# Reordering a kernel's start: x products ahead of the first weight products, w_in by blocks of columns, two blocks begun on half of x, and two transposes in a shared buffer

## The chip, the core and the metric

The kernel runs on one core of a Trainium2 chip. The time is the device time of one execution in microseconds (us), as a median of several runs. TensorE (PE in the profile) multiplies matrices out of SBUF into PSUM; VectorE (DVE), ScalarE (ACT) and GpSimd (POOL) work on elements; SyncE (SP) issues most transfers (DMA). GpSimd issues the transfers that cast from f32 to bf16. In the traces here each engine does its work in the order of its own queue, and that order is what this study is about.

## The reference, cut to what matters

```python
q_s = softmax(q over its last axis);  k_s = softmax(k over the sequence)   # q, k, v: (8, 8, 576, 64)
kv  = einsum('bhsd,bhse->bhde', k_s, v)
x   = einsum('bhsd,bhde->bhse', q_s, kv)  # seen as 4608 tokens x 512
h   = x @ w_in                            # w_in: 512 x 2048
g   = h + sin(alpha * h)**2 / alpha
out = g @ w_out                           # w_out: 2048 x 512, out: 4608 x 512 f32
```

The kernel goes through nine token blocks of 512. Eight batches of 576 tokens feed them, so the first token block needs batch 0 except its ninth row group, and the second token block needs that group and most of batch 1. Within a token block there are 16 column blocks of 128 columns of w_in, numbered `ni` from 0; below, "block" with such a number is one of these. "The first w_in products" are those of the first token block.

## The kernel before

What the change and the argument touch. First the loads that GpSimd issues at the start: v's second half for batch 0, then w_in, first by rows:

```python
load0(GP, "v", v, 1, 0, 5)
load0(GP, "v", v, 1, 5, 9)
load_win(0, 512, slice(0, 2))       # columns 0-511, half of the rows: two transfers
load_win(0, 512, slice(2, 4))       # the other half of the rows
for c0 in (512, 1024, 1536):
    load_win(c0, c0 + 512)          # 512 columns, all rows, two transfers each
for c in range(2):
    load_wout(c)
```

Then TensorE's order for the first token block. `mm_h(t, ni, _, k0, k1)` adds row groups k0 to k1 of w_in to block ni; `attn_chunk` is an x product; `xT` is x, transposed, in bf16:

```python
kv_mm(0, 1, ps_e, split=True)       # kv of batch 0, second half
kv_norm(0, 1, 2)                    # VectorE: kbd, which the x products read
for ni in range(4):
    mm_h(0, ni, None, 0, 1)         # four w_in products on the first quarter of x
xp = [ps_e.tile(...) for _ in range(2)]
for e in range(2):                  # second half's x products, then casts to xT
    attn_chunk(0, 2 + e, 0, 8, xp[e])
    (DVE_CP, ACT_CP)[e](xT[:, 2 + e, 0:MF], xp[e])
for ni in range(4):
    mm_h(0, ni, None, 1, 2)         # the second quarter
# ... then each block's remaining row groups, its sine, its square and g
```

And the place, after the first token block, where batch 1 is prepared between the output products (`take(os, n)` emits n of them):

```python
for ii in range(2):
    q_transpose(1, ii, ps_e, DVE_CP)
tp = ps_e.tile([128, 2, 128], BF16, name="tp", tag="a")      # a third transpose buffer
for ii in range(2):
    nc.tensor.transpose(tp[:, ii], A["qe", 0][:, 8, ...], identb)
DVE_CP(A["qT", 0][:, :, 8], tp)
cast_v(1, [ACT_CP, DVE_CP])         # VectorE casts v's second half here ...
take(os, 6)
xp = ps_e.tile([128, 4, P], F32, name="xp", tag="a")
# ... the ninth row group's x products ...
DVE_CP(xT[:, :, 8 * P:9 * P], xp)   # ... ahead of this copy, and of an output copy inside take()
take(os, 2)
kv_mm(1, 0, ps_e, split=True);  kv_norm(1, 0, 1);  take(os, 2)
kv_mm(1, 1, ps_e, split=True);  kv_norm(1, 1, 2);  take(os, 1)
```

The softmax here doesn't subtract the row's maximum and nothing guards it: scores larger than these inputs give would overflow.

Of the kernel before, what the change touches and what calls it, by code (L numbers as in the profile page):

```python
# [16 lines left out]
BF16 = mybir.dt.bfloat16  # L17
# [6 lines left out]
def kernel(  # L24
# [14 lines left out]
    nc = tc.nc  # L39
# [5 lines left out]
    J = 9  # L45
# [20 lines left out]
    identb = singles.tile([128, 128], BF16, name="identb")  # L66
    xT = singles.tile([128, 4, NT], BF16, name="xT")
    win = singles.tile([128, 4, d_ff], BF16, name="win")
# [10 lines left out]
    win_v = moe_w_in.rearrange("(x c d) n -> x d c n", x=2, c=4)  # L79
# [5 lines left out]
    def load(name, t, b, halves=False, eng=nc.sync, gate=None):  # L85

        st = stage.tile([128, 4, J, D], F32, name=f"st_{name}", tag="st")
        for ii in range(2) if gate else ():
            gate(st[:, ii, 0, 0:1], zero)
        view = src_view(t, b)  # L90
        flat = st.rearrange("p i j d -> p i (j d)")
        if halves:
            for ii in range(2):
                eng.dma_start(out=flat[:, ii::2], in_=view[:, ii::2])
        else:
            eng.dma_start(out=flat, in_=view)
        staged[name, b] = st
# [3 lines left out]
        load("k", k, b)  # L101
        load("v", v, b)

    def load_win(c0, c1, ks=slice(0, 4)):
        n = slice(c0, c1)
        for x in range(2):
            nc.gpsimd.dma_start(out=win[64 * x:64 * x + 64, ks, n], in_=win_v[x][:, ks, n])

    def load_wout(c):
        nc.gpsimd.dma_start(out=wout[:, 4 * c:4 * c + 4, :], in_=wout_v[:, 4 * c:4 * c + 4, :])  # L110


    A = {}

    def exp_to(dst, src, iis=range(2)):
        for ii in iis:
            nc.scalar.activation(dst[:, :, ii * 128:(ii + 1) * 128].rearrange("p j (x d) -> p x j d", x=2),  # L117
                                 src[:, ii::2], AX.Exp)
# [10 lines left out]
    def exp_k(b):  # L129
        A["ke", b] = att2.tile([128, J, 4 * D], BF16, name="ke")  # L130
        exp_to(A["ke", b], staged["k", b])
# [43 lines left out]
    def kv_norm(b, i0=0, i1=2):  # L175

        kt, m = kbd[b % 2], i1 - i0
        kvr = small.tile([128, 2, 2, 2], F32, name="kvr")[:, :, 0:m]
        src = A["kvp", b][:, :, i0 * 130:i1 * 130].rearrange("p e (ii x c) -> p e ii x c", ii=m, x=2)
        nc.vector.reciprocal(kvr, src[:, :, :, :, D])  # L180
        for x in range(2):
            r = slice(64 * x, 64 * x + 64)
            nc.vector.tensor_tensor(kt[r, :, i0:i1, r], src[r, :, :, x, 0:D],
                                    kvr[r, :, :, x].unsqueeze(3).to_broadcast([64, 2, m, D]), op=ALU.mult)

    def q_tile(b):
        if ("qT", b) not in A:
            A["qT", b] = att2.tile([128, 2, J, 128], BF16, name="qT")
        return A["qT", b]

    def q_transpose(b, ii, pool, eng):
        tp = pool.tile([128, 16, 128], BF16, name="tp", tag="a")
        q_transpose_ii(b, ii, 0, J, tp)
        eng(q_tile(b)[:, ii], tp[:, 0:J])

    def q_transpose_ii(b, ii, j0, j1, tp):

        for j in range(j0, j1):
            nc.tensor.transpose(tp[:, j - j0], A["qn", b][:, ii, j], identb)
# [35 lines left out]
    def mm_h(t, ni, wide=None, k0=0, k1=4):  # L235

        if ni == 0 and k0 == 0:
            G[t] = gpool.tile([128, nN, MF], BF16, name="g")
        if k0:
            hp = HP[t, ni]  # L240
        elif wide and (ni in (4, 5, 9, 10, 14, 15) if t == 0 else ni % 6 in (4, 5)):
            hp = wide()
        else:
            hp = ps_h.tile([128, MF], F32, name="hp", tag="h")
        HP[t, ni] = hp
        for ki in range(k0, k1):
            nc.tensor.matmul(hp, win[:, ki, ni * 128:(ni + 1) * 128],  # L247
                             xT[:, ki, t * MF:(t + 1) * MF], start=(ki == 0), stop=(ki == 3))
        return hp

    def sine(t, ni, hp, sq):
        s = spool.tile([128, MF], F32, name="s")
        nc.scalar.activation(s, hp, AX.Sin, scale=alpha_sb[:, ni:ni + 1])  # L253
        if sq == "A":
            nc.scalar.activation(s, s, AX.Square)  # L255
        elif sq == "P":
            nc.gpsimd.tensor_tensor(s, s, s, op=ALU.mult)  # L257
        else:
            nc.vector.tensor_tensor(s, s, s, op=ALU.mult)
        return s  # L260
# [19 lines left out]
    ACT_CP, DVE_CP, GP_CP = nc.scalar.copy, nc.vector.tensor_copy, nc.gpsimd.tensor_copy  # L280
# [4 lines left out]
    def load0(eng, n, t, ii, j0=0, j1=J):  # L285
        eng.dma_start(out=staged[n, 0][:, ii::2, j0:j1].rearrange("p i j d -> p i (j d)"),
                      in_=src_view(t, 0)[:, ii::2, j0 * D:j1 * D])
# [14 lines left out]
    ps_e = ES.enter_context(tc.tile_pool(name="ps_e", bufs=2, space=PSUM, reuse_waits="tile"))  # L302
# [14 lines left out]
    GP_CP(singles.tile([128, 1], F32, name="held"), staged["k", 0][:, 0, 0, 0:1])  # L317
    load0(GP, "v", v, 1, 0, 5)
    load0(GP, "v", v, 1, 5, 9)
    load_win(0, 512, slice(0, 2))  # L320
    load_win(0, 512, slice(2, 4))
    for c0 in (512, 1024, 1536):
        load_win(c0, c0 + 512)
    for c in range(2):
        load_wout(c)

    def warm_up(n):

        for _ in range(n):
            nc.tensor.matmul(warm, identb, A["qe", 0][:, 0:4, 0:128], start=True, stop=True)  # L330




# [25 lines left out]
    ACT_CP(xT[:, 1, 0:MF], xp[1])  # L360
    kv_mm(0, 1, ps_e, split=True)
    kv_norm(0, 1, 2)
    for ni in range(4):
        mm_h(0, ni, None, 0, 1)
    xp = [ps_e.tile([128, 2, MF], F32, name="xp", tag="a")[:, 0] for _ in range(2)]
    for e in range(2):
        attn_chunk(0, 2 + e, 0, 8, xp[e])
        (DVE_CP, ACT_CP)[e](xT[:, 2 + e, 0:MF], xp[e])
    for ni in range(4):
        mm_h(0, ni, None, 1, 2)  # L370

    def h_slot(t, ni, sq, lag, wide=None):
        hp = mm_h(t, ni, wide, 2 if ni < (4, 2, 0)[min(t, 2)] else 0)
        lag.append((t, ni, hp, sine(t, ni, hp, sq)))

    def flush(lag, keep):
# [23 lines left out]
    with ES:  # L400
        def lent():
            return ps_e.tile([128, 2, MF], F32, name="hh", tag="a")[:, 0]

        def load_q8():
            for ii in range(2):
                load0(nc.sync, "q", q, ii, 8, 9)

        late = {4: load_q8, 6: lambda: load("q", q, 1, halves=True, gate=DVE_CP), 8: lambda: load_wout(2),
                10: lambda: load_wout(3), 13: lambda: load("k", k, 1, halves=True, gate=DVE_CP)}
        for ni in range(nN):  # L410
            h_slot(0, ni, "DPPAPPAPPPAPPAPP"[ni], lag, lent)
            flush(lag, 1)
            if ni in late:
                late[ni]()
        flush(lag, 0)

        accs = [ps_h.tile([128, dm], F32, name="hp", tag="h") for _ in range(4)]
        os = o_quad(0, accs, [DVE_CP, ACT_CP, DVE_CP, ACT_CP])
        take(os, 46)
        exp_to(A["qe", 0][:, 8:9], staged["q", 0][:, :, 8:9])  # L420
        exp_q(1)
        load("v", v, 1, halves=True)
        load_batch(2)
        norm_q8()
        norm_q(1, [GP, V])
        exp_k(1)
        for ii in range(2):
            q_transpose(1, ii, ps_e, DVE_CP)
        tp = ps_e.tile([128, 2, 128], BF16, name="tp", tag="a")
        for ii in range(2):  # L430
            nc.tensor.transpose(tp[:, ii], A["qe", 0][:, 8, ii * 128:(ii + 1) * 128], identb)
        DVE_CP(A["qT", 0][:, :, 8], tp)
        cast_v(1, [ACT_CP, DVE_CP])
        nc.scalar.activation(zero, zero, AX.Sin)
        take(os, 6)
        xp = ps_e.tile([128, 4, P], F32, name="xp", tag="a")
        for c in range(4):
            attn_chunk(0, c, 8, 9, xp[:, c])
        DVE_CP(xT[:, :, 8 * P:9 * P], xp)
        take(os, 2)  # L440
        kv_mm(1, 0, ps_e, split=True)
        kv_norm(1, 0, 1)
        take(os, 2)
        kv_mm(1, 1, ps_e, split=True)
        kv_norm(1, 1, 2)
        take(os, 1)

        c0 = J * P
        for ii in range(2):
            xp = ps_e.tile([128, 2, 512], F32, name="xp", tag="a")[:, :, 0:7 * P]  # L450
            for e in range(2):
                attn_chunk(1, 2 * ii + e, 0, 7, xp[:, e])
            (ACT_CP, DVE_CP)[ii](xT[:, 2 * ii:2 * ii + 2, c0:c0 + 7 * P], xp)
            take(os, 2)
        take(os)
        load("q", q, 3)
        load("k", k, 3)

        for ki in range(2):
            for ni in range(2):  # L460
                mm_h(1, ni, lent, ki, ki + 1)
        for ni in range(nN):
            h_slot(1, ni, SQ[ni], lag, lent)
            flush(lag, 1)
        cast_v(2, [GP_CP, GP_CP])
        flush(lag, 0)
# [38 lines left out]
    c0 = J * 2 * P  # L505
# [33 lines left out]
    for t in range(3, nT):  # L539
# [13 lines left out]
        for ni in range(nN):  # L553
            hp = mm_h(t, ni)
# [46 lines left out]
```

## Time and profile before

| | before |
|---|---|
| median of the first three runs | 289.59 us (289.34 to 290.04) |
| span of the profiled execution | 287.8 us |
| TensorE busy | 273.6 us, 95% |
| first w_in product of the second token block | 48.24 us |
| span left from there | 239.55 us |

The last two rows are the measure that I use throughout. I look for the change's effect ahead of the second token block's first product. I call its start S.

Two lines of VectorE's timeline (start, length, engine, line, operation):

```profile
43.76 0.68 DVE L273 COPY o<-hp 128x512 f32<-128x512 f32 x1
44.36 0.41 DVE L439 CAST xT<-xp 128x256 bf16<-128x256 f32 x1
```

Both stand in VectorE's queue behind the cast of v's second half. That cast could not begin before v had landed at 43.06 us.

### The profile page before, as it was taken

How to read it: one execution, taken by the hardware profiler on the slowest of the kernel's cores; microseconds unless marked ns; L12 is line 12 of the kernel's file. 1: busy time of each engine (PE TensorE's matmuls, PEld its weight loads, DVE VectorE, ACT ScalarE, POOL GpSimd, SP SyncE). 2: the span in 40 equal slices, each digit the busy share in tenths (PEclk: the TensorE clock that was granted, in tenths of full speed). 3: DMA queues.
4: the chain of work that ended last, by engine and by line, in shares of the span. 5: the costliest groups of instructions: out<-in, count | busy, mean ns of one | idle time of the engine just before them, and what ended most of it. 6: DMA issues, size and time to landing. Idle time of an engine off the chain costs nothing.

```text
span 287.8 us, 4238 instructions
## 1 busy us (share of the span) xinstructions
PE 273.6 (95%) x1541; PEld 130.9 (45%) x1569; DVE 189.1 (66%) x285; ACT 225.8 (78%) x319; POOL 81.9 (28%) x77
## 2 busy tenths in 40 slices
PE   2898999999999999999999999999999999999995
PEld 1443454444454445444544454445444444444443
DVE  3947876889958567856776676747674555555412
ACT  4878855999579999899889988999877777777500
POOL 2869520675675662005300440022000000000000
PEclk9999999999999999999999999999999999999999
DMA  7999999945899957119910990115111111111142
GB/s 245 307 204 235 270 396 408 319 159 143 206 144 407 403 178 138 38 38 353 295 23 22 328 344 7 38 39 130 25 39 36 36 36 39 36 36 38 40 109 73
DMA packets 37541, 45.77 MB, mean 159 GB/s; under 512 B 16512, under 2 KB 20880, under 8 KB 37520
## 3 DMA queue, kind: packets, MB, share of 16 engines
q1 hardware_dynamic: 32848, 40.57, 46.1%
q0 software_dynamic: 4480, 4.79, 9.5%
q8 instruction: 12, 0.20, 0.3%
q10 hardware_dynamic: 192, 0.14, 0.2%
q14 instruction: 9, 0.07, 0.1%
HBM read 36.71 MB, written 9.44 MB: 160 GB/s over the span
## 4 chain that ended last, share of the span: by engine, by line
PE 85%; DMA 5%; DVE 3%; POOL 3%; issue 2%; ACT 1%; SPq 0%
PE hp L247 36%; PE op L267 34%; PE hp L267 5%; PE hh L247 2%; PE kvp L170 2%; DMA win<-in_moe_w_in_dram 2%; DMA st_k<-in_k_dram 2%; PE xp L219 2%; POOL s L257 1%; DMA qT<-qn 1%; ACT s L253 1%; PE op L571 1%; PE op L247 1%; DVE qs L149 1%; PE xp L227 1%
## 5 line engine op out<-in xcount | busy, mean ns | idle before, releaser
L263 DVE SCALAR_TENSOR_TENSOR g<-s,inva_sb,hp 128x512 bf16<-128x512 f32 x130 | 96.2, 745 | 64.0 <-ACT s L255 54.2
L247 PE MATMUL hp<-xT,win 128*128 128x512 bf16 x512 | 129.3, 379 | 1.9 <-DMA win<-in_moe_w_in_dram 1.4
L267 PE MATMUL op<-wout,g 128*128 128x512 bf16 x479 | 121.8, 379 | 1.1 <-issue 0.5
L253 ACT ACTIVATE s<-hp,alpha_sb 128x512 f32<-128x512 f32 x130 | 87.5, 683 | 26.9 <-PE hp L247 24.6
L247 PEld LDWEIGHTS <-win 128*128 128x128 bf16 x576 | 56.1, 98 | 70.0 <-issue 2.1
L267 PEld LDWEIGHTS <-g 128*128 128x128 bf16 x560 | 54.0, 98 | 61.6 <-issue 0.7
L255 ACT ACTIVATE s<-s 128x512 f32<-128x512 f32 x111 | 69.9, 630 | 3.5
L151 POOL TENSOR_TENSOR qn<-qe,qs 128x1152 bf16<-128x1152 bf16 x12 | 25.3, 2127 | 72.7 <-DVE qs L145 63.2
L257 POOL TENSOR_TENSOR s<-s 128x512 f32<-128x512 f32 x30 | 31.5, 1060 | 24.9 <-ACT s L253 24.4
L273 DVE COPY o<-op 128x512 f32<-128x512 f32 (+2 forms) x33 | 22.1, 668 | 9.6 <-PE op L267 5.5
L117 ACT ACTIVATE ke<-st_k 128x1152 bf16<-128x1152 f32 x16 | 17.9, 1151 | 4.2 <-DMA st_k<-in_k_dram 4.2
L117 ACT ACTIVATE qe<-st_q 128x1152 bf16<-128x1152 f32 (+2 forms) x18 | 18.0, 1048 | 2.6 <-DMA st_q<-in_q_dram 2.6
L144 DVE TENSOR_REDUCE qs<-qe 128x36 f32<-128x2304 bf16 x5 | 12.8, 2552 | 8.7 <-ACT qe L117 8.6
L136 POOL CAST vb<-st_v 128x1152 bf16<-128x1152 f32 x12 | 13.6, 1162 | 9.9 <-DMA st_v<-in_v_dram 9.9
L267 PE MATMUL hp<-wout,g 128*128 128x512 bf16 x62 | 14.7, 379 | 0.2 <-issue 0.2
L222 DVE CAST xT<-xp 128x512 bf16<-128x512 f32 (+1 forms) x18 | 13.4, 742 | 0.0
L247 PE MATMUL hh<-xT,win 128*128 128x512 bf16 x39 | 9.5, 379 | 0.8 <-DVE g L263 0.7
L170 PEld LDWEIGHTS <-ke 64*128 64x128 bf16 x288 | 8.2, 93 | 4.5 <-issue 1.8
L117 ACT ACT_TABLE_LOAD x7 | 9.0, 1283 | 1.3 <-PEq L585 1.2
L170 PE MATMUL kvp<-vb,ke 64*128 64x130 bf16 x288 | 9.9, 216 | 0.0
L149 DVE TENSOR_REDUCE qs<-qe 128x18 f32<-128x1152 bf16 (+1 forms) x6 | 7.7, 1286 | 2.4 <-ACT qe L117 2.4
L219 PE MATMUL xp<-qT,kbd 128*128 128x256 bf16 (+1 forms) x40 | 8.2, 286 | 0.4 <-DVE xT L222 0.3
(75 smaller groups left out, 119.0 us busy)
## 6 DMA issues: line engine op xcount, KB each, us to landing
out_dram<-o SPq DMA_DIRECT2D x70, 128.0 KB, 2.4
st_q<-in_q_dram SPq DMA_DIRECT2D x6, 1152.0 KB, 6.5
st_k<-in_k_dram SPq DMA_DIRECT2D x6, 1152.0 KB, 8.3
st_v<-in_v_dram SPq DMA_DIRECT2D x6, 1152.0 KB, 10.1
st_k<-in_k_dram SPq DMA_DIRECT2D x4, 576.0 KB, 7.3
wout<-in_moe_w_out_dram POOLq DMA_DIRECT2D x4, 512.0 KB, 11.0
st_v<-in_v_dram SPq DMA_DIRECT2D x3, 576.0 KB, 9.0
win<-in_moe_w_in_dram POOLq DMA_DIRECT2D x6, 256.0 KB, 8.0
```

The source lines that it names most:

```text
L117: nc.scalar.activation(dst[:, :, ii * 128:(ii + 1) * 128].rearrange("p j (x d) -> p x j d", x=2), src[:, ii::2], AX.Exp)
L136: engs[ii](vv[:, 2 * ii:2 * ii + 2, :, 0:D], staged["v", b][:, ii::2])
L151: engs[ii % len(engs)].tensor_tensor(qn[:, ii, 0:j1].rearrange("p j (x d) -> p j x d", x=2), qe[:, ii], part.unsqueeze(3).to_broadcast([12 ...
L170: nc.tensor.matmul(kvp[:, e, ii * 130:(ii + 1) * 130], ke[r, j, ii * 128:(ii + 1) * 128], vt[r, j, ii * 130:(ii + 1) * 130], start=(j == 0 ...
L219: nc.tensor.matmul(xp[:, e, 0:n], kt[:, e, ii], qT[:, ii, j0:j1, e * 64:(e + 1) * 64], start=True, stop=True)
L247: nc.tensor.matmul(hp, win[:, ki, ni * 128:(ni + 1) * 128], xT[:, ki, t * MF:(t + 1) * MF], start=(ki == 0), stop=(ki == 3))
L253: nc.scalar.activation(s, hp, AX.Sin, scale=alpha_sb[:, ni:ni + 1])
L255: nc.scalar.activation(s, s, AX.Square)
L257: nc.gpsimd.tensor_tensor(s, s, s, op=ALU.mult)
L263: nc.vector.scalar_tensor_tensor(G[t][:, ni], in0=s, scalar=inva_sb[:, ni:ni + 1], in1=hp, op0=ALU.mult, op1=ALU.add)
L267: nc.tensor.matmul(acc, G[t][:, ni, j * 128:(j + 1) * 128], wout[:, ni, :], start=(ni == 0), stop=(ni == nN - 1))
L273: eng(o[:, cols], acc)
```

## The change

It means to fill TensorE's 1.41 us of idle time at 13.6 us: (part 1) the x products, whose inputs are ready, go ahead of the w_in products, whose data has not landed; (part 2) w_in arrives so that two blocks can be computed in full after two transfers; (part 3) only two blocks, not four, are begun before all of x is there. The hunk at the end (part 4) saves one PSUM buffer for two small transposes.

```diff
-    load_win(0, 512, slice(0, 2))
-    load_win(0, 512, slice(2, 4))
-    for c0 in (512, 1024, 1536):
-        load_win(c0, c0 + 512)
+    for c0, c1 in ((0, 256), (256, 512), (512, 1024), (1024, 1536), (1536, 2048)):
+        load_win(c0, c1)
...
-    for ni in range(4):
-        mm_h(0, ni, None, 0, 1)
     xp = [ps_e.tile([128, 2, MF], F32, name="xp", tag="a")[:, 0] for _ in range(2)]
     for e in range(2):
         attn_chunk(0, 2 + e, 0, 8, xp[e])
         (DVE_CP, ACT_CP)[e](xT[:, 2 + e, 0:MF], xp[e])
-    for ni in range(4):
-        mm_h(0, ni, None, 1, 2)
+    for ki in range(2):
+        for ni in range(2):
+            mm_h(0, ni, None, ki, ki + 1)
...
-        for ii in range(2):
-            q_transpose(1, ii, ps_e, DVE_CP)
-        tp = ps_e.tile([128, 2, 128], BF16, name="tp", tag="a")
+        q_transpose(1, 0, ps_e, DVE_CP)
+        tp = ps_e.tile([128, 16, 128], BF16, name="tp", tag="a")
+        q_transpose_ii(1, 1, 0, J, tp)
         for ii in range(2):
-            nc.tensor.transpose(tp[:, ii], A["qe", 0][:, 8, ii * 128:(ii + 1) * 128], identb)
-        DVE_CP(A["qT", 0][:, :, 8], tp)
+            nc.tensor.transpose(tp[:, J + ii], A["qe", 0][:, 8, ii * 128:(ii + 1) * 128], identb)
+        DVE_CP(A["qT", 1][:, 1], tp[:, 0:J])
+        DVE_CP(A["qT", 0][:, :, 8], tp[:, J:J + 2])
```

Cut: two signatures that follow from this (`load_win` loses its row argument, and `h_slot` begins blocks 0 and 1 at the third row group, the others at the first).

More of the change, by code (lines that the diff above doesn't have):

```diff
@@ L102, in load_batch, with load_win @@
         load("v", v, b)
-    def load_win(c0, c1, ks=slice(0, 4)):
+    def load_win(c0, c1):
         n = slice(c0, c1)
         for x in range(2):
-            nc.gpsimd.dma_start(out=win[64 * x:64 * x + 64, ks, n], in_=win_v[x][:, ks, n])
+            nc.gpsimd.dma_start(out=win[64 * x:64 * x + 64, :, n], in_=win_v[x][:, :, n])
     def load_wout(c):
@@ L368 @@
         (DVE_CP, ACT_CP)[e](xT[:, 2 + e, 0:MF], xp[e])
-    for ni in range(4):
-        mm_h(0, ni, None, 1, 2)
+    for ki in range(2):
+        for ni in range(2):
+            mm_h(0, ni, None, ki, ki + 1)
     def h_slot(t, ni, sq, lag, wide=None):
-        hp = mm_h(t, ni, wide, 2 if ni < (4, 2, 0)[min(t, 2)] else 0)
+        hp = mm_h(t, ni, wide, 2 if t < 2 and ni < 2 else 0)
         lag.append((t, ni, hp, sine(t, ni, hp, sq)))
```

## The prediction

> **What bounds the kernel now.** I read the page first: its busy line and its chain line.
>
> ```profile
> PE 273.6 (95%) x1541; PEld 130.9 (45%) x1569; DVE 189.1 (66%) x285; ACT 225.8 (78%) x319; POOL 81.9 (28%) x77
> ...
> PE 85%; DMA 5%; DVE 3%; POOL 3%; issue 2%; ACT 1%; SPq 0%
> ```
>
> TensorE is busy for 273.6 of 287.8 us and makes up 85% of the chain that ended last. Its 512-column matmuls follow each other every 0.216 us (start to start in the trace; the 379 ns of a row is the pipelined length). Only time in which TensorE stands idle, about 14 us, can be won. So I looked through the trace for steps between matmul starts above 0.23 us. After the warm-up matmuls nearly all of them lie before 49 us: 1.41 us at 13.6, 0.73 us at 28.0 and 0.35 us at 41.6. After that TensorE runs almost without a break to the end. The change touches the first and the third. What counts is how much earlier the second token block's products start (48.24 us, the row at L247 after the output quad), because everything later is TensorE's own length and moves with it.
>
> The chain of waits for 0 to 36 us (start, length, what), then the timeline (the same, with the idle time before in brackets), show the first place:
>
> ```profile
> 8.53 6.36 DMA win<-in_moe_w_in_dram
> ...
> 16.48 2.59 PE hp L247 x12
> ...
> 28.76 1.89 PE hh L247 x8
> ```
>
> ```profile
> 15.02 1.02 PE L247 MATMUL hp<-xT,win 128*128 128x512 bf16 x3 [1.41 <-DMA win<-in_moe_w_in_dram]
> ...
> 15.88 0.59 PE L227 MATMUL xp<-qT,kbd 128*128 128x512 bf16 x2
> ...
> 18.91 1.89 PE L247 MATMUL hh<-xT,win 128*128 128x512 bf16 x8
> ```
>
> The second w_in transfer lands at 8.53 + 6.36 = 14.89 us; TensorE, done with kv at 13.60, waits for it. The two x products (L227) stand behind four w_in products, though their kbd is ready at 14.59 (VectorE row at L183: 14.00 + 0.59). But look at 18.91: that is the first product of block 4, which reads columns 512 to 1024. The trace has their two transfers landing at 17.44 and 18.76. TensorE arrives there with 18 matmuls from 15.02 (18 x 0.216 = 3.89, so 18.91), just 0.15 us after the data. The start is matched to the DMA already.
>
> The DMA itself is full in this stretch (view by stretches; the last column is GB/s as written in bf16, and twice that is read in f32):
>
> ```profile
> 16.00:18.00 2.00, 2.00 (x11) 0.88 (x9) 0.69 (x1) 0.77 (x2) 1.31 (x2) 1.00 1.23 204
> 18.00:20.00 2.00, 2.00 (x11) 0.84 (x10) 1.44 (x2) 2.00 (x4) 0.84 (x1) 1.00 1.24 205
> ```
>
> That is about 410 GB/s read, and it stays so to 52 us (the 38 to 48 stretch has 407 GB/s). So any transfer behind w_in lands when the bytes ahead of it are through.
>
> The second place, VectorE and TensorE around 42 us:
>
> ```profile
> 41.93 0.27 PE L431 MATMUL tp<-identb,qe 128*128 128x128 bf16 x2 [0.35 <-DVE qT L194]
> ...
> 43.08 0.76 DVE L136 CAST vb<-st_v 128x1152 bf16<-128x1152 f32 x1 [0.35 <-DMA st_v<-in_v_dram]
> ...
> 45.86 0.18 DVE L180 RECIPROCAL kvr<-kvp 128x4 f32<-128x4 f32 x1 [0.35 <-PE kvp L170]
> ...
> 47.36 1.09 DVE L453 CAST xT<-xp 128x896 bf16<-128x896 f32 x1 [0.70 <-PE xp L227]
> ```
>
> TensorE waits 0.35 us for a free PSUM buffer, VectorE waits 0.35 us for batch 1's v to land (43.06), and later 0.35 us for TensorE's kv.
>
> **What the Trainium skill says.** "DMA: Bandwidth & Descriptors", section "Why small descriptors are slow (HBM only)": a packet carries a fixed overhead of about 3 cycles beside its 32-byte beats. The trace agrees roughly: the two loads of 256-byte q rows (64 KB each) land 0.22 us apart, 298 GB/s, where rows of 2 KB and more run at about 410; by the page's cycles it would be 410 x (8/11)/(64/67), about 312. The same page, "Issuing engines are not separate DMA queues", says that transfers of all issuing engines share the same 16 DMA engines; the full stretches above agree. "PSUM — Partial Sum Buffer", Terms, gives 8 banks: here ps_h holds 4 and ps_e 2 buffers of 2 banks, all of them, so the third transpose tile can only wait; the 0.35 us at 41.93 is that wait.
>
> **The change part by part.**
>
> 1. The second half's two x products go ahead of all w_in products. They start when kbd and the second qT (ScalarE copy, done 14.63) are there, about 14.68, and end their issue at 14.68 + 2 x 0.216 = 15.11. The casts to xT, now at 16.30 and 16.52, come at about 15.1 and 15.3 and end by 15.9. TensorE saves 0.43 us of order at best: the first w_in product could start at 15.11.
>
> 2. w_in comes as 256 columns for all rows, twice, then 512 as before. Bytes and number of transfers stay (10), but the first four have 256 rows of 1 KB each where they had 128 of 2 KB. In the trace they cost 0.64 us each after the first (14.22, 14.89, 15.53, 16.16). By the page's overhead 2 x (32+3) = 70 cycles take the place of 67: 4.5%, 4 x 0.64 x 0.045 = 0.12 us in all (estimate). The worse case: a 2 KB packet with the cast took 98 ns, without it (q rows) 84, so 14 ns per packet may be fixed; 4 x 128 more packets x 14 ns / 16 engines = 0.45 us more. I take a delay D of 0.2 us for all that lands behind, with 0 to 0.6 possible.
>
> 3. Two blocks begin on half of x, not four. Blocks 0 and 1 need only the first two transfers (before: 14.89; after about 15.0), so TensorE starts at about 15.1, runs eight products to 16.85, has the next two transfers by 16.4, and comes to block 4 at 15.1 + 16 x 0.216 = 18.57. There its columns land at 18.76 + D = 18.96; with the 0.13 us from landing to matmul that the trace shows (14.89 to 15.02) it goes on at 19.1, against 18.91. The 0.34 us of lead becomes a wait of about 0.5 us. ScalarE gets its first sine at about 16.6 and not 17.81, but from block 4 on one block comes each 4 x 0.216 = 0.86 us, and block 7's sine (23.33 before) needs block 7's product at about 22.7 and the two ScalarE items ahead of it. So the chain ScalarE, GpSimd (24.08), VectorE (27.96), TensorE (28.76) starts again where it did, within 0.3 us either way. Worth of parts 1 to 3 at 30.5 us: 0.0, from -0.35 (D = 0) to +0.3 (D = 0.6).
>
> 4. The two transposes of the ninth row go into the second transposes' buffer. No wait for VectorE's copy: the step of 0.566 us at 41.93 becomes about 0.06. TensorE is 0.5 us earlier there. VectorE's work is the same three copies. But VectorE's next work, the v cast, is held by the landing at 43.06 + D, and then it has no gap: cast, output copy, xT copy, reciprocal, two kbd products end at 45.51 + D. The second reciprocal (45.86 before) can start then: 0.35 - D earlier, not 0.5. The x products of batch 1 follow it, and so does 48.24.
>
> Sum: the gain at 48.24 is the smaller of (part 4 plus parts 1 to 3, 0.5 + 0.0) and (0.35 - D) = 0.15 us with D = 0.2. All else is unchanged: 289.59 - 0.15 = 289.44; I say 289.4.
>
> **The rivals.**
>
> A. The first gap is a real gain: 0.4 to 0.9 us of the 1.41 us come off the end. For it: it is the largest idle stretch of TensorE after warm-up, and GpSimd, which is full from 24.08 on, could start a microsecond earlier. Against it: block 4 has only 0.15 us of slack to its transfer, and 42 to 46 us hangs on v's landing, which is set by bytes. It would make 288.7 to 289.1.
>
> B. The finer rows cost more than I think, or the first transfer's slow start (1.61 us from 12.61 to 14.22, where later ones take 0.64) grows with twice the packets. Everything queued behind, v for batch 1 too, lands 0.6 us or more later. For it: packets in that start took up to 181 ns. Against it: bytes are equal, and the slow start looks like one of a new region, as q's has it too (338 ns in its first packets). It would make 289.8 to 290.2.
>
> C. The transfers are hidden and only part 4 counts in full, 0.5 us: this needs v to land early, which the 0.35 us wait at 43.08 speaks against. 289.1.
>
> **Range and chances.** D from 0 to 0.6 gives gains of 0.35 to -0.25, so 289.24 to 289.84. The runs before spread over 289.34 to 290.04, so I add 0.2 above; rival A widens the low side to 288.7. Range 288.7 to 290.0. 2% is 5.8 us, more than all TensorE idle time touched here (1.41 + 0.73 + 0.35), so faster by over 2% and slower by over 2% get 0.01 each.
>
> **What the changed profile would show.** Part 1: x products at about 14.7 and xT casts ended by 15.9. Part 2: the four first w_in transfers landing 0.64 to 0.8 us apart, and columns 512 to 1024 later than 18.76. Part 3: a new TensorE wait of some 0.3 to 0.6 us for w_in at block 4, and a wait for VectorE's g near 28 us still there. Part 4: no gap at the ninth row's transposes, but v still awaited near 43 us and the second reciprocal near 45.5 to 45.9. Wrong would be: no wait at block 4, with TensorE's products of the first token block ended before 30.0; or v landing at another time than D says; or the start of the second block's products at 48.24 moved by more than 0.5 us.

## The result, and the profile after

The changed kernel took 289.15 us (median of six, 288.68 to 289.51), the kernel before 289.6 us in its six runs beside it. The ratio is 0.9981, with a 95% interval of 0.9967 to 0.9995; timed again later it was 0.9984 (0.9964 to 1.0004). Ratios are the mean time of one kernel's fast runs over that of the other's fast runs of the same rounds, so they are not quite the ratio of the medians quoted. The verdict is "same" at 2%; a gain of about half a microsecond, just clear of the noise in the first timing and not in the second.

The profiled span went from 287.8 to 287.7 us. That single execution lost 0.3 us again between 168 and 178 us; the second trace of the same kernel did not, and had 287.3.

The changed kernel's timeline of the start, TensorE's rows:

```profile
14.45 0.60 PE L227 MATMUL xp<-qT,kbd 128*128 128x512 bf16 x2 [0.96 <-DVE kbd L183]
...
15.11 3.40 PE L247 MATMUL hp<-xT,win 128*128 128x512 bf16 x15
...
18.35 1.89 PE L247 MATMUL hh<-xT,win 128*128 128x512 bf16 x8
...
27.83 1.89 PE L247 MATMUL hh<-xT,win 128*128 128x512 bf16 x8 [0.68 <-DVE g L263]
...
29.55 2.75 PE L267 MATMUL hp<-wout,g 128*128 128x512 bf16 x12
```

TensorE no longer waits for w_in at all. What it waits for at 14.45 is VectorE's kbd. At 18.35 it comes to block 4 without a gap: columns 512 to 1024 had landed at 16.27 and 17.48 us (before: 17.44 and 18.76). The wait for VectorE's g near 28 us is still there (0.68 us, before 0.73), but all of it comes earlier: the output products start at 29.55 where they started at 30.48. That is a lead of 0.93 us.

The lead is not in the result. Here is where it goes, the same view at 42 us:

```profile
42.86 0.69 PE L170 MATMUL kvp<-vb,ke 64*128 64x130 bf16 x18 [0.26 <-ACT vb L136]
...
43.09 0.77 DVE L136 CAST vb<-st_v 128x1152 bf16<-128x1152 f32 x1 [1.29 <-DMA st_v<-in_v_dram]
...
43.77 0.69 DVE L273 COPY o<-hp 128x512 f32<-128x512 f32 x1
...
44.37 0.41 DVE L436 CAST xT<-xp 128x256 bf16<-128x256 f32 x1
...
44.84 0.69 PE L170 MATMUL kvp<-vb,ke 64*128 64x130 bf16 x18 [0.75 <-DVE xT L436]
...
45.56 0.18 DVE L180 RECIPROCAL kvr<-kvp 128x4 f32<-128x4 f32 x1
...
47.95 2.32 PE L247 MATMUL hp<-xT,win 128*128 128x512 bf16 x10
```

VectorE stands still for 1.29 us (before 0.35) until v's second half has landed, at 43.07 us, where it landed at 43.06 before. TensorE then waits 0.26 us for ScalarE's cast of v's first half and 0.75 us for the xT copy behind VectorE's cast (the second half's kv takes the PSUM buffer that this copy empties: all these tiles share the two buffers of `ps_e`). The bracket names "DVE xT L436", not v. One has to follow VectorE's queue two rows up to see that the copy is late because the cast ahead of it waited for a transfer. S moved from 48.24 to 47.95, 0.29 us.

The chain of waits for 0 to 50 us says it in one line. Before, the v transfer was not on the chain at all:

```profile
32.12 10.95 DMA st_v<-in_v_dram
43.07 0.02 issue
43.09 0.77 DVE vb L136
43.86 0.59 DVE o L273
44.45 0.34 DVE xT L436
44.79 0.04 issue
44.84 0.69 PE kvp L170 x18
```

### The profile page after: what moved, and what is told of

It is laid out like the page before. It is cut to its first block, busy times and chain, and to the rows that moved or that the text cites. A ratio compares the mean times of both kernels' runs of the same rounds, so it can differ in the third digit from the quotient of the medians.

```text
span 287.7 us, 4238 instructions
## 1 busy us (share of the span) xinstructions
PE 273.6 (95%) x1541; PEld 131.3 (46%) x1569; DVE 189.2 (66%) x285; ACT 226.0 (79%) x319; POOL 81.8 (28%) x77
## 4 chain that ended last, share of the span: by engine, by line
PE 76%; DMA 9%; DVE 5%; ACT 3%; POOL 3%; issue 3%; SPq 0%; POOLq 0%; DVEq 0%; ACTq 0%
PE hp L247 34%; PE op L267 30%; DMA qT<-qn 4%; DMA st_v<-in_v_dram 4%; PE hh L247 2%; PE kvp L170 2%; PE xp L219 2%; POOL qn L151 1%; POOL s L257 1%; ACT s L253 1%; PE warm L328 1%; DMA st_q<-in_q_dram 1%; PE op L568 1%; PE op L247 1%; DVE qs L144 1%
## 5 line engine op out<-in xcount | busy, mean ns | idle before, releaser
L257 POOL TENSOR_TENSOR s<-s 128x512 f32<-128x512 f32 x30 | 31.5, 1060 | 25.8 <-ACT s L253 25.4
L136 POOL CAST vb<-st_v 128x1152 bf16<-128x1152 f32 x12 | 13.6, 1162 | 10.6 <-DMA st_v<-in_v_dram 10.6
```

The lines of the kernel that those rows point to most:

```text
L257: nc.gpsimd.tensor_tensor(s, s, s, op=ALU.mult)
```

## The experiments

**The theory** (A in the expectations): S is set by whichever comes last of two paths. One is TensorE's own: the start of the output products plus its work up to S. The other is the landing of batch 1's v plus VectorE's queue behind it. Before, TensorE came last by a little; the change speeds up TensorE's path by much more than that little, and v comes last. **Rivals:** the gain comes from the start directly, or from part 4 alone, and v has nothing to do with it. (The letters of the expectations are not those of the prediction's rivals.)

Eleven runs. First the change taken apart in two halves, and a kernel that takes the wait for v out of VectorE's way.

**1. Part 4 alone.** The edit is the last hunk of the change, on the kernel before.

> The kernel before with part 4 alone (the ninth row's two transposes go into the second transposes' buffer). Theory A (gain = the smaller of TensorE's lead and a cap that the landing of v at 43.07 us sets through VectorE's queue): TensorE is 0.5 us earlier after the transposes, but the second block's products start only about 0.3 us earlier than 48.24, about 47.95, so part 4 alone gives all of the gain: 0.3 us, ratio near 0.999. Theory B (the gain comes from the start, where TensorE is 0.93 us earlier at 29.55): no gain here, ratio 1.000, second block at about 48.2.

Measured: 289.68 us against 289.9, ratio 0.9996 (0.9970 to 1.0022). In the trace TensorE's step at the transposes is gone, and a new wait stands at the second kv:

```profile
43.37 0.68 PE L170 MATMUL kvp<-vb,ke 64*128 64x130 bf16 x18
...
45.31 0.69 PE L170 MATMUL kvp<-vb,ke 64*128 64x130 bf16 x18 [0.72 <-DVE xT L440]
...
48.42 0.81 PE L247 MATMUL hp<-xT,win 128*128 128x512 bf16 x3
```

S is 48.42, not the expected 47.95, because v happened to land at 43.54 in this execution. 43.54 + 4.88 = 48.42, and in the changed kernel 43.07 + 4.88 = 47.95. So the number missed, and the reason for the miss is the theory's own. The ratio cannot tell a gain of 0.3 us from none.

**2. The change without part 4.** The edit is the change minus its last hunk.

> The changed kernel without part 4 (order of the x products, column blocks and half-x start of two blocks alone). Theory A: TensorE ends the first block's products about 0.9 us earlier (29.55 and not 30.48), waits again 0.35 us at the ninth row's transposes, and meets the same cap, so the second block starts at about 47.95 again: 0.3 us gain, ratio near 0.999. Theory B: the same, since the start is the cause. Theory C (part 4 is what counts): no gain, ratio 1.000, second block at 48.2. The two w_in transfers of columns 512 to 1024 should land at about 16.3 and 17.5 as in the changed kernel if the early landing belongs to the column blocks, and at about 17.4 and 18.8 if it was chance.

Measured: 289.24 us against 289.9, ratio 0.9974 (0.9955 to 0.9993), as good as the whole change. S was 48.01, with v at 43.13: again 4.88 later. Part 4 is therefore not what counts (theory C falls). The question about w_in was answered by chance: columns 512 to 1024 landed at 17.32 and 18.64, though up to there the program is the same as the changed kernel's, where they landed at 16.27 and 17.48. Even so TensorE did not wait at block 4, since it was late itself: its x products began only at 15.08, as v of batch 0 had landed at 13.13, not 12.11.

**3. The changed kernel with VectorE's cast of v behind the two copies.**

```diff
-        cast_v(1, [ACT_CP, DVE_CP])
+        cast_v(1, [ACT_CP, lambda o, i: None])
 ...
         DVE_CP(xT[:, :, 8 * P:9 * P], xp)
+        cast_v(1, [lambda o, i: None, DVE_CP])
```

> The changed kernel with VectorE's cast of the second half of batch 1's v put behind the output copy and the ninth row's xT copy in VectorE's queue. Theory A: the two copies no longer stand behind a cast that waits for v, TensorE's 0.75 us wait at 44.84 for the xT copy falls away, kv of the second half starts at about 43.9 and the second block's products at about 47.2 and not 47.95: 0.7 us less than the changed kernel, ratio to before about 0.996. Rival (the cap is not VectorE's queue behind v): the same as the changed kernel, ratio 0.998.

Measured: 288.69 us (288.47 to 289.19) against 289.9, ratio 0.9957 (0.9938 to 0.9976). The total is as theory A said. (The changed kernel without the late cast was not timed in the same rounds; its ratios are 0.9981 and 0.9984.) S in the trace is 47.78, not 47.2: this execution started slowly (output products from 30.38), and TensorE came last, 17.40 us from there to S. That is not all its own length, though the forecasts below take it for that. The second kv could only start when the late cast had ended, at 43.86 + 0.75 = 44.61:

```profile
43.37 0.69 PE L170 MATMUL kvp<-vb,ke 64*128 64x130 bf16 x18
...
43.86 0.75 DVE L136 CAST vb<-st_v 128x1152 bf16<-128x1152 f32 x1
...
44.67 0.69 PE L170 MATMUL kvp<-vb,ke 64*128 64x130 bf16 x18
```

It follows the first kv by 1.30 us, where the kernel before has 1.15 (43.98 and 45.13). So 0.15 us of the 17.40 is a wait for the cast, and 17.25 is TensorE's own.

**4. The late cast on the kernel before.** The same edit on the other kernel.

> The kernel before with only the cast put late as in the run ahead of this one. Theory A: here TensorE, not v, comes last (the xT copy runs at 44.36 because its x products come at 43.3), so a cast behind it starts at 44.8, kv of the second half is held from 45.13 to about 45.6, and the kernel is the same or up to 0.4 us slower: ratio 1.000 to 1.0015. Rival (a late cast is a gain by itself): 0.7 us faster, ratio 0.9975.

Measured: 289.72 us, ratio 1.0003 (0.9976 to 1.0030). The late cast alone brings nothing that shows. That fits theory A, which says that TensorE is last there; the rival's 0.9975 lies just outside the interval. In the trace the second kv follows the first by 1.31 us, again held by the late cast.

**5. and 6. Both kernels again,** unchanged, for second traces.

> The kernel before, unchanged, for a second trace. The four traces so far show the first loads landing up to a microsecond apart from run to run. Theory A: the second half of v still lands at 43.0 to 43.5 us, and the second block's products start at that landing plus 4.9 us or later, whichever of v and TensorE comes last (5.18 us in the first trace, where TensorE came last). The first w_in transfer should land 1.2 to 2.0 us after the last piece of v, as in the three traces with row blocks (1.61, 2.01, 1.16), if that slow start belongs to the row blocks.

> The changed kernel, unchanged, timed again. Expected ratio 0.998 as before, between 0.997 and 0.9995. Theory A: the second block's products start 4.9 us after v's second half has landed, wherever that is, with waits of TensorE for v of 0.3 to 1.0 us in all between 42 and 45 us. If the first w_in transfer's short start (0.67 us here, 0.39 and 0.89 in the two other traces with column blocks) belongs to the column blocks it shows again; if it was chance it may be 1.2 to 2.0 us.

Measured: the kernel before had S = 47.92 here and v at 43.04, 4.88 apart: in this execution its output products started at 29.80 rather than 30.48, and v came last for it too. In the same trace TensorE, early at block 4, waits there for w_in:

```profile
18.60 1.89 PE L247 MATMUL hh<-xT,win 128*128 128x512 bf16 x8 [0.36 <-DMA win<-in_moe_w_in_dram]
```

The changed kernel was timed at 0.9984 (0.9964 to 1.0004), S = 47.78, v at 42.90, again 4.88 apart. The first w_in transfer landed 1.18 us after v's last piece by rows and 0.83 us by columns. With the other traces that is 0.5 to 2.0 us (rows of w_in, five traces) against 0.4 to 0.9 us (columns, eight). The two ranges meet, so whether the blocks of columns shorten this start stays open.

**7. The order alone** (part 1):

```diff
     kv_norm(0, 1, 2)
-    for ni in range(4):
-        mm_h(0, ni, None, 0, 1)
     xp = [...]
     for e in range(2):
         attn_chunk(0, 2 + e, 0, 8, xp[e]) ...
+    for ni in range(4):
+        mm_h(0, ni, None, 0, 1)
     for ni in range(4):
         mm_h(0, ni, None, 1, 2)
```

> The kernel before with part 1 alone: the second half's x products ahead of the w_in products, all four blocks still begun on half of x, w_in still by rows. Theory A: x products start at about 14.6 to 14.9 instead of 15.9, the w_in products follow without a gap after their landing near 14.9, TensorE comes to block 4 about 0.4 us earlier, just when columns 512 to 1024 land (18.7), and waits for them up to 0.4 us; v then sets the second block's start as before: ratio 0.999 to 1.000. Rival (the order is what the gain comes from): ratio 0.998 or less.

Measured: 289.88 us against 290.01, ratio 0.9994 (0.9974 to 1.0014), as theory A said; the rival's 0.998 or less is not excluded. The profiled execution had a very slow start (k's second half landed at 12.12, before 10.56). The x products began only at 15.78, so the wait for w_in at block 4 that was expected had no occasion. TensorE came last: output products at 31.25, S = 49.01, which is 17.76 later, as in the first trace of the kernel before (48.24 - 30.48 = 17.76).

**8. The blocks of columns alone** (part 2), the first hunk of the change on the kernel before.

> The kernel before with the column blocks alone (part 2), TensorE's order as before: four blocks begun on the first quarter of x, so the first products of blocks 2 and 3 need the fourth transfer (about 16). Theory A: TensorE does two products, stands until about 16, and ends the first block's products about 0.7 to 1.1 us later (31.2 to 31.5), which is more than the 0.3 us that v leaves: 0.4 to 0.8 us slower, ratio 1.0015 to 1.003. Rival (the column blocks alone bring the gain, by the shorter start of the transfers): ratio 0.998.

Measured: 289.83 us, ratio 0.9990 (0.9971 to 1.0009), so not slower as expected, and the total is a miss for theory A's number; the rival's 0.998 lies inside the interval and is not excluded. The trace shows the wait that was expected, for the fourth transfer:

```profile
14.44 0.59 PE L247 MATMUL hp<-xT,win 128*128 128x512 bf16 x2 [0.70 <-DMA win<-in_moe_w_in_dram]
15.96 0.38 PE L247 MATMUL hp<-xT,win 128*128 128x512 bf16 x1 [0.94 <-DMA win<-in_moe_w_in_dram]
```

and S at 48.54 = 30.79 + 17.76, TensorE last. The output products started at 30.79, only 0.3 us after the first trace's 30.48: I had expected 31.2 to 31.5, because the two waits together are about as long as the one that they replace (1.41 us). The brackets add up to 1.64 us, but a matmul's record is missing ahead of 15.96 (four w_in products stand before the x products, three are recorded, and two weights were loaded from 15.72 on); with its 0.22 us taken off, the waits are 1.42 us.

**9. The changed kernel with v made later on purpose.** A load of 288 KB that nobody reads is put ahead of batch 1's v:

```diff
+        spare = singles.tile([128, J * D], F32, name="spare")
+        nc.sync.dma_start(out=spare, in_=src_view(q, 1)[:, 0])
         load("v", v, 1, halves=True)
```

> The changed kernel with one load more, of 288 KB into a spare tile that nothing reads, put in the queue just ahead of batch 1's v. At 410 GB/s that is 0.72 us of transfers. Theory A, in the form that eight of the nine traces fit within 0.1 us: the second block's products start at the later of (end of the first block's products + 17.4 us) and (landing of v's second half + 4.88 us), and in the changed kernel v comes last. So v lands at about 43.7, the products start at about 48.6, and the whole kernel is 0.7 us slower than the changed one: ratio to before about 1.0005 where the changed kernel has 0.998. Rival (v is not what comes last, the load is hidden): 0.998.

Measured: 290.52 us, ratio 1.0015 (0.9988 to 1.0041), against 0.998 without the load (timed in other rounds), and 1.0005 expected. v landed at 43.91 and S was 48.80, 4.89 later. The rival predicted 0.998 and falls. The waits grew where the theory has them:

```profile
43.72 0.69 PE L170 MATMUL kvp<-vb,ke 64*128 64x130 bf16 x18 [1.27 <-ACT vb L136]
...
45.68 0.69 PE L170 MATMUL kvp<-vb,ke 64*128 64x130 bf16 x18 [0.74 <-DVE xT L438]
```

The first kv waits 1.27 us (0.26 in the changed kernel). The second still waits about as long as there, since the first has moved too.

**10. and 11. Past the changed kernel.** Run 10 has the late cast, and GpSimd issues two w_out loads later, so that its issues no longer hold the square of block 9; run 11 is run 3 again.

```diff
-        late = {4: load_q8, 6: ..., 8: lambda: load_wout(2),
-                10: lambda: load_wout(3), 13: ...}
+        late = {4: load_q8, 6: ..., 9: lambda: load_wout(2),
+                12: lambda: load_wout(3), 13: ...}
```

> The late cast of VectorE as in the third run, and besides GpSimd issues the third and fourth loads of w_out after blocks 9 and 12 and not after 8 and 10, so that the square of block 9 is no longer behind an issue of 0.8 us and TensorE's 0.68 us wait for VectorE's g near 28 us falls away. With the late cast it is TensorE that comes last (47.78 = 30.38 + 17.40 in that trace), so 0.4 to 0.7 us should come off unless v's landing + 4.2 us (the earliest with the late cast, an estimate from its trace) stops it: ratio to before 0.994 (0.993 to 0.996), where the late cast alone had 0.9957. Rival (the w_out loads land too late, or the wait comes back at another buffer): 0.996 or more.

> The changed kernel with the late cast, again, beside the run ahead. Theory A: in a run with a quick start (first block's products ended at 29.5) the second block's products start 17.4 us after it, near 47.0, at most at v's landing + 4.2; in a slow one near 47.8. Ratio to before 0.9957 again, between 0.994 and 0.9975.

Measured: run 10 took 288.53 us, ratio 0.9957 (0.9926 to 0.9988); run 11 took 288.74 us (288.51 to 288.94), ratio 0.9950 (0.9924 to 0.9975). So the late cast's gain repeats, and the later w_out issue adds nothing that shows. In run 10's trace the wait for g near 28 us is gone and the output products start at 28.54, a full microsecond earlier. It is spent on two other waits:

```profile
40.83 1.02 PE L267 MATMUL hp<-wout,g 128*128 128x512 bf16 x4 [0.65 <-DMA wout<-in_moe_w_out_dram]
...
42.84 0.69 PE L170 MATMUL kvp<-vb,ke 64*128 64x130 bf16 x18 [0.44 <-ACT vb L136]
...
47.11 1.24 PE L247 MATMUL hp<-xT,win 128*128 128x512 bf16 x5
```

The fourth w_out load now lands at 40.78, and TensorE waits for it: the rival's "load lands too late". Behind it TensorE waits again for ScalarE's cast of v's first half. For run 11, VectorE's rows show what the late cast does:

```profile
42.30 0.69 DVE L273 COPY o<-hp 128x512 f32<-128x512 f32 x1 [0.29 <-PE hp L267]
42.91 0.41 DVE L436 CAST xT<-xp 128x256 bf16<-128x256 f32 x1
43.29 0.76 DVE L136 CAST vb<-st_v 128x1152 bf16<-128x1152 f32 x1
```

The copies run in the time in which VectorE used to stand still, and the cast starts as v lands (43.27). S is 47.28, 4.01 us after that landing, where it was 4.88 with the early cast. But VectorE's cast no longer holds TensorE here; v's first half does, which ScalarE casts:

```profile
43.02 0.69 PE L170 MATMUL kvp<-vb,ke 64*128 64x130 bf16 x18 [0.20 <-ACT vb L136]
...
44.17 0.69 PE L170 MATMUL kvp<-vb,ke 64*128 64x130 bf16 x18
```

The second kv follows the first by the unheld 1.15 us. The first half landed at 41.77, and S is 5.51 us later; in run 10 it landed at 41.60, and S is again 5.51 us later.

**All traces in one table.** TensorE's path is the start of the output products plus 17.76, or plus 17.25 with part 4. v's path is the landing of its second half plus 4.88; with the late cast it is the landing of its first half (41.48, 41.69, 41.77 and 41.60 in runs 3, 4, 11 and 10) plus 5.51. The lengths are read from these traces themselves; the test is that each serves all its traces (17.76 three, 4.88 six, 5.51 two). No trace shows 17.25 unheld. It is 17.40 less the 0.15 in run 3, and also 17.76 less the 0.51 that part 4 saves at the transposes (from the first transpose to the ninth row's 1.52 us in the kernel before, 1.01 in run 1).

| trace | output products | v's second half landed | TensorE's path | v's path | S measured |
|---|---|---|---|---|---|
| before | 30.48 | 43.06 | 48.24 | 47.94 | 48.24 |
| before again (5) | 29.80 | 43.04 | 47.56 | 47.92 | 47.92 |
| part 4 alone (1) | 30.39 | 43.54 | 47.64 | 48.42 | 48.42 |
| order alone (7) | 31.25 | 43.23 | 49.01 | 48.11 | 49.01 |
| column blocks alone (8) | 30.79 | 42.84 | 48.55 | 47.72 | 48.54 |
| changed | 29.55 | 43.07 | 46.80 | 47.95 | 47.95 |
| changed again (6) | 29.37 | 42.90 | 46.62 | 47.78 | 47.78 |
| without part 4 (2) | 30.18 | 43.13 | 47.94 | 48.01 | 48.01 |
| v later (9) | 29.39 | 43.91 | 46.64 | 48.79 | 48.80 |
| late cast (3) | 30.38 | 42.95 | 47.63 | 46.99 | 47.78 |
| late cast on the kernel before (4) | 30.15 | 43.14 | 47.91 | 47.20 | 48.06 |
| late cast again (11) | 29.76 | 43.27 | 47.01 | 47.28 | 47.28 |
| late cast, w_out later (10) | 28.54 | 43.03 | 45.79 | 47.11 | 47.11 |

The later of the two paths gives S within 0.01 us in eleven traces. In the other two, runs 3 and 4, TensorE comes last with a late cast, and S is 0.15 us behind its path: that is the hold of the second kv shown under run 3. The landing of v hardly depends on the kernel (42.84 to 43.54 where nothing was added), and the start of the output products does so only on average. Up to there the program is the kernel before's in four traces (30.48, 29.80, 30.39 and 30.15, runs 1 and 4 included; mean 30.21) and the changed one's in six (29.55, 29.37, 30.18, 30.38, 29.39 and 29.76, with runs 2, 3, 9 and 11; mean 29.77). So the start's lead is 0.44 us in the mean, in ranges that overlap; the 0.93 us of the first pair is twice that.

## Why the prediction was right or wrong

The range held, and 289.4 was 0.25 us above what came. The number alone decides nothing between the stories: 289.15 lies 0.05 us from rival A's 288.7 to 289.1 and from rival C's 289.1. Of the prediction's own signs of being wrong, two came: no wait at block 4 with an early end of the first token block's products (the output products start at 29.55), and v landing at another time than D says. Point by point:

**What bounds the kernel:** right. Everything behind S was TensorE's own length, to within 0.6 us in thirteen traces.

**Part 1:** right. The x products began at 14.45 and 14.28 in the two traces (14.68 predicted), and the casts to xT ended by 15.7.

**Part 2:** the small size was right. The first four w_in transfers land 0.68 and 0.67 us apart by columns in the two traces, and 0.65 and 0.64 by rows (means over three steps), 0.03 us each (over all traces 0.67 to 0.74 and 0.64 to 0.79, so no more than these pairs shows it). That is about the 4.5% that I took from the packet overhead of "DMA: Bandwidth & Descriptors", section "Why small descriptors are slow (HBM only)"; the 14 ns per packet of the worse case do not show. But D, the delay of all that lands behind, was set at 0.2 us, and v landed at 43.07 and 42.90 against 43.06 and 43.04, so D was 0.0 to -0.1.

**Part 3 is the step that failed.** It said that TensorE's "0.34 us of lead becomes a wait of about 0.5 us" at block 4, and that parts 1 to 3 are worth 0.0 at 30.5 us. In neither trace of the changed kernel, nor in runs 2, 3, 9, 10 and 11, which start as it does, is there a wait for w_in at block 4. TensorE's lead at the output products is 0.93 us against the first trace of the kernel before and 0.25 us against its second, 0.44 us in the mean of all. The chain over ScalarE, GpSimd and VectorE, which was to start again "where it did, within 0.3 us", let TensorE go on at 27.83 where it had been 28.76. I had taken the landings of one trace, 17.44 and 18.76, for fixed. The second of them was anywhere from 17.41 to 18.76 over the traces, and with the same program up to there at 17.48 and at 18.64; 18.96 was expected. Where TensorE is early and the transfer is not, the wait does come: the kernel before has it in its second trace (0.36 us at 18.60, run 5). When the transfer is late, batch 0's v ahead of it in the queue can be late as well, and TensorE hangs on that v. In this, rival A had the better account of the start.

**Part 4 and the sum:** the mechanism was right, and it is why the total came out near. The prediction let the gain at S be the smaller of TensorE's lead and 0.35 - D, the cap from VectorE's queue behind v. The second reciprocal was to start at 45.5 to 45.9 and started at 45.56. With D at 0.0 in place of 0.2 the cap is 0.35, and S moved by 0.29 us. The last 0.05 is a detour that the prediction did not have: VectorE's own work ended at 45.50, but the reciprocal reads the second kv, and that stood behind the xT copy until 44.84. So the wrong 0.0 for parts 1 to 3 did no harm: 0.93 us from the start and 0.51 us from part 4 (0.5 predicted) made 1.44 us of lead for TensorE, and it gave back 1.15 us in the waits for v (18.40 us from output products to S in place of 17.25), which leaves the 0.29. Rival A, that 0.4 to 0.9 us "come off the end", saw the lead but not where it is given back; run 3 shows that with the cast moved the gain grows. By the timings the gain goes with the start: run 2, which leaves part 4 out, has it (0.9974), and run 1, part 4 alone, shows none (0.9996). Rival C (part 4 in full, 0.5 us, a ratio of 0.9983) lies inside run 1's interval; what speaks against it is run 2 and the wait for v in run 1's trace. Rival B (the finer rows delay v by 0.6 us or more) did not come: v landed as before, and the first w_in transfer's slow start did not grow (0.67 and 0.83 us, before 1.61 and 1.18).

**What stays open:** the timed gain is about 0.5 us, more than the 0.29 us of the pair of first traces, and the second traces differ by 0.14 us only. A reading that fits the table is that in executions with a slow start the kernel before has TensorE last, sometimes by far, and the change takes that away. Each trace is a single execution, so this is argued, not shown. Why v lands at 43 us even when w_in lands 1.2 us earlier is open too. In the first pair that lead of w_in is gone by its last transfer (23.88 before, 23.84 after), but in runs 10 and 11 the last one landed at 22.72 and 22.92, and v still at 43.03 and 43.27.

## What to carry to other kernels

When an early gap is closed, follow the freed engine to the next place where it meets something that the change does not move, here a transfer whose landing did not follow the start; what can be gained is the distance to that, not the length of the gap. Then look at what stands behind the wait in the same queue: moving one cast two places down, behind copies that did not need the transfer, took the changed kernel from 0.998 to 0.995 or 0.996 (not timed side by side), about as much again as the whole change; on the kernel before, where something else came last, it brought nothing that shows (1.0003). Take landing times from at least two traces before an argument hangs on tenths of a microsecond.

## What the Trainium skill lacked or had wrong

- No page gives the scatter of the first loads from run to run. "DMA: Bandwidth & Descriptors" gives latencies without their spread; here the fifth load that SyncE issues (k's second half), with the same loads ahead of it, landed anywhere from 10.02 to 12.12 us over thirteen traces.
- "Runtime: NRT & Kernel Launch", section "Instruction fetch mechanics", says that instructions are fetched in 16 KiB blocks, at a cost "mostly hidden". The traces list one such 16 KB packet among the DMA packets of each start, 0.89 to 0.98 us long. In the five traces where it began between 21.0 and 22.4 us, w_in's last transfer landed 1.75 to 2.48 us after the one ahead of it; in the eight where it began later, 1.3 to 1.4 us. No run moved the fetch alone, so this is a coincidence of times, not a proof.
